# One core, adaLN with linear attention and an MLP: block 1's rows transposed by VectorE and DRAM

## The chip, the cores and the metric

The kernel runs on one core of a Trainium2 chip. The metric is the device time of one execution in microseconds (us), the lower the better. It is measured several times; the median counts. Names of engines in the profile: PE (TensorE), DVE (VectorE), ACT (ScalarE), POOL (GpSimd) and SP (SyncE, whose queue issues the kernel's DMAs). PSUM is the memory in which PE leaves its products, in eight banks.

## The reference

The input x has 2048 rows of 512. Everything is fp32. Cut to what matters:

```python
mod = (silu(c) @ w_mod).reshape(1, 6, 1, 512)          # sa, ca, ga, sb, cb, gb
h = layernorm(x) * (1 + ca) + sa
q, k, v = split(h @ wqkv)                              # 32 heads of 16
pq, pk = q @ w_phi, k @ w_phi                          # per head, 16x16
phi = lambda p: concat([softmax(p), softmax(-p)])      # 32 features a head
kv = phi(pk).T @ v;  z = phi(pk).sum(rows)             # over all 2048 rows
o = (phi(pq) @ kv) / (phi(pq) @ z + 1e-6)
x = x + ga * (o @ wo)
h = layernorm(x) * (1 + cb) + sb
x = x + gb * (gelu(h @ w1 + b1) @ w2 + b2)             # F = 1376
```

## The kernel before, in words

**Tiling.** The rows are eight blocks of 256, each held as two halves of 128 rows. PE contracts over partitions, so a block's normalised rows h have to stand transposed, channels on the partitions: 512 channels are four chunks of 128. Every fp32 product is made from three cheaper ones (`mm3`): each operand is split into a high part and a low part, and high·high, high·low and low·high are added up in PSUM. So a 128×512 product over four chunks is twelve matmuls. The transposed block is therefore two tiles, hT0 (high, made by ScalarE) and hT1 (low, made by GpSimd from the affine tile hf minus hT0, in two halves of two chunks each, `h_finish`).

**Stages.** The head (some 24 us) loads the weights, folds the small matrices w_phi into the weights of q and k (`fold` on PE, read out of PSUM by ScalarE as `wq` or `wk` high and by VectorE as the low part), forms the first modulation vectors (`wm`, `prod`, `affine`) and transposes block 0. Then, block by block, the projections pk, pq and pv, the key features ek, and the accumulation pkv of kv over all rows, until about 137 us. Then kv is closed (kvT, zp), the first two blocks go through attention (qp and qT: transposed features; po: attention's product; pw: times wo), and from 190 us on the MLP runs on pairs of blocks (pg: times w1, g: its gelu, py: times w2) with the attention of the next two blocks in between.

**Two ways to transpose.** `ln1_apply(b)` normalises a block and `h_transpose(b)` transposes it and applies the modulation. Which way is taken is set by the constant NT.

- Blocks 0 and 1 (b < NT): PE transposes eight 128×128 tiles into two PSUM banks (tiles named hp), and the affine step reads the banks. For block 1 the affine step is `h_affine`, four ScalarE instructions into hf.
- Blocks 2 to 7 (b >= NT): VectorE transposes the 32×32 blocks of each half (two instructions, xt to nb), four DMAs store nb to a DRAM tensor nt_dram in an order that completes the transpose, one DMA loads it back with the channels on the partitions (hd), and four ScalarE instructions make hf from hd with the affine step.

**What sets the order.** Each engine runs its instructions in program order, and that order is written out. The functions of the kernel don't issue anything: they leave their instructions in queues, one for each step and engine (class `Later`, lines 220 to 241), and the table ISSUE then lists, for each of the kernel's parts, which queue gives its next instruction. So all instructions carry the line 217 in the profile, and tiles tell them apart. Loads and stores go through SP's one queue in the order of that table: an issue that has to wait for its data holds up all issues behind it. A second table, SLOTS, gives each tile its buffer: nineteen numbered buffers of 4 KB a partition, eight PSUM banks, and pairs of small ones. A tile whose buffer was used by another one waits until the last reader of that one is done.

Of the kernel before, what the change touches and what calls it, by code (L numbers as in the profile page):

```python
# [47 lines left out]
    "32eg91ai750d4gf6cf8ehcd187ga30203dh540b52ca0i999hba44571a6i7b8gag3fii0729f4c2fe569d1ehch8d61bg59801c"  # L48
    "7bda51ii68d72i6cc6g44bh676i1ia4e7ah24igi3g908053d78d90d850883efef7g7bbd7b5d5edbfe4id3f8g6f302hbab1ca"
    "gc1d035356268688c6ac633e1e6c0d3h2dffgahfi9f5df3d02gg340052aa2h0f05gc7532d6ggcbhd8g",  # L50
    "bank":
    "3534201077650761644611400766431302014372076341621740122107154521543753631407720101023324531207674567"
    "54567546767640763123523132153152524724605130311550313053514273015015610",
    "st6a": "11101010",
    "sta": "00010101",
    "vea": "01101101",
    "rsa": "01110001",
    "nma": "10111111",
    "dz": "001110010",
    "mxk": "1010101110101010",  # L60
    "smk": "0110010111011011",
    "rck": "1010010111101101",
    "mxq": "10110010",
    "smq": "00000000",
    "rcq": "10100020",
    "den": "00101110",
    "rd": "10111011",
    "st6b0": "10100110",
    "stb0": "10111101",
    "veb0": "10010101",  # L70
    "rsb0": "11001011",
    "st6c0": "01000110",
    "stc0": "10111100",
    "vec0": "00100100",
    "rsc0": "00101000",
    "nmc0": "10010111",
    "st6b1": "11110101",
    "stb1": "10000110",
    "veb1": "11111110",
    "rsb1": "00010101",  # L80
    "st6c1": "10000001",
    "stc1": "10111010",
    "vec1": "00110110",
    "rsc1": "00100101",
    "nmc1": "00000111",
# [3 lines left out]
-init.v -init.p dq.s db.s x0.s dk.s x1.s dk.s dm.s dk.s dm.s si.a bd.v dq.s fq.p s0.v -w2.p oq.a s0.v -w3.p si.v  # L89
-init.v s0.v dk.s s0.v si.v fk.p si.v s0.v dm.s s0.v oq.v s0.g sr.p s1.v n0.v n0.v s1.v n0.a fq.p s1.v n0.v ok.a  # L90
sr.a fk.p s1.v ok.v x.s m.g dm.s m.v h0.p dv.s ok.a fk.p s1.v bg.s s1.v m.v oq.a ok.v m.a m.g m.v h0.p ok.a -w4.p
f.v +x.s s1.g ok.v fq.p m.a n1.v f.a m.v fk.p n1.a f.v dv.s n1.v f.v m.g oq.a pf.p oq.v f.a n1.a f.v ++x.s m.v ok.a
pf.p m.a m.v oq.v m.g f.v h.p s.v f.a fq.p h.a m.v m.a h.p f.v pf.p bg.s h.a s.v +bg.s h.a s.v +bg.s s.v oq.a s.v
m.v s.v f.v s.g +++x.s oq.v f.a bg.g vs.a f.v q1.p n.v +s.v h.a ok.v vs.a n.v vs.v pf.p n.a vs.g ++s.v n.a q0.p k1.v
bg.a n.v n.v +bg.g bg.v n.s pv0.p +s.v n.s f.a +bg.g ++s.v q1.a n.s +bg.a +s.v ++s.v n.s k1.v f.g +bg.a +bg.s ++s.v
++s.v +s.v +s.v ++s.v k0.v f.a pv1.p k0.v f.g +++s.v n.s k1.v ++++x.s +bg.g +s.v k0.v k0.v
""",
    """
pk1.p s.g +s.g n.v n.v bg.v n.a bg.g -k1.v n.a bg.s ++++x.s ++s.v -q0.a +bg.s pk0.p bg.v -k1.a e.v h.a h.a ++s.v
++s.v n.v -k0.a q1.p +n.v bg.v -v1.a +bg.g ++s.v n.v bg.a e.v h.a n.s +n.a n.s -k0.v f.a pv0.p n.s -v0.a f.g n.s h.a  # L100
# [25 lines left out]
pk1.p -k0.v -k1.a --bg.g -k0.v -k1.v pk0.p h.a -v0.v v1.v k1.v -v0.a -k0.g +d0.s h.a k1.v ----e.s h.a h.a f.a -m0.p
--bg.g k0.v f.a -m1.p k1.v m0.p k1.v pv1.p +w1.s -k1.v +w1.s k1.a --v1.v f.g -v1.v k0.v v1.v k0.v f.g k1.v
""",
    """
pk1.p -v1.a -----e.v --k1.g ---bg.a --v1.a -k0.v -k0.a -k1.v pk0.p ----v0.v k1.v +lp0.s -k1.g -k0.v --v1.v --bg.g  # L130
-k0.v -m1.p w1.a k0.v m1.p k1.v -pv0.p w1.a d0.s v1.v k0.v w1.s -k0.g k0.v v0.v k1.v k0.v -v0.v pv0.p w1.g k0.a
-v0.a k0.v w1.g k0.v pv1.p k1.v v0.a +a0.v k1.a v0.v v1.v k1.v k0.g q1.p v1.a k1.v w1.a +a0.v k1.g ---v0.v m0.p
+a0.g m2.p m3.p w1.g kT.a d1.s d1.s z.p z.a kf.p +a0.g q0.p z.a q1.a a0.g q1.p a1.g a0.v -----e.v a0.v --bg.s q2.p
q1.a a1.g +a0.a kf.v a0.v q0.a a1.v q2.p a0.g a1.v a0.g a0.g +a0.g a0.v +a0.v q0.p a1.g a0.g a1.g a0.v a1.g a0.g
a1.v q4.p q0.a --bg.s x0.s q2.a a1.g +a0.g t01.p a1.g +a0.a t01.p t00.p t00.p +a0.v q4.p q4.a a1.g t01.a +a0.v t00.a
t01.a t00.a +a0.g q2.a o01.p q2.s o00.p w1.s t10.p q0.s o00.a t11.p o01.a +a0.g o00.v t10.p t11.p o01.v w00.p t10.a
+a0.v q4.a t11.a q4.s --bg.g +a0.v t10.a t11.a w1.a o11.p la00.v o10.p la00.a -bg.g w01.p x1.s o10.a la00.v o11.a
o10.v la00.v o11.v +a0.g -bg.a la00.v la00.v la00.g w11.p +a0.g la01.v +a0.g w1.g lb00.v la01.a +a0.v la01.v lb00.v
w10.p la11.v w1.s q1.s la01.v lb00.v la11.a la01.v la01.v +lp1.s la01.g w2.s la11.v -bg.g lb01.v q3.p la11.v lb01.v
la10.v +a0.g lb01.v la11.v la10.a lb00.v lb01.v la11.v lb00.g lb01.g q3.p la10.v la11.g lc00.v la10.v lc01.v la10.v  # L140
lc01.a la10.v la10.g lb11.v +a0.g lc00.a lb10.v q3.a y0.p q3.a lb11.v y0.p y0.a +a0.g lb10.v q3.s y0.a y0.v --bg.a
lb10.v y0.v
""",
    """
u0.p -w1.a -lb11.v -lb10.v -lb11.v a0.v -lb10.g -lb11.g u0.p a0.v ---bg.g -lc10.v -lc11.v a0.v a0.s -lc10.a a1.v
a0.s u0.p -lc11.a a0.s a1.v a0.s a1.g -y1.p -y1.p -y1.a u0.p --v0.v a0.v a1.g -y1.a -y1.v a0.s a1.g -y1.v a1.a a0.s
u1.p a0.s a1.g a0.s u1.p -w1.g +lp0.s u.a u.a u1.p u.a u.v a0.s u.a a1.v a0.s -w2.g d.p -w1.s u.a d.p u.v u.a d.p
u.v d.p a1.g a1.a d.p d.p -w2.a a1.v d.p a1.g d.p a1.v d.p x0.s a1.v u1.p -w2.g a1.v o01.p o00.p +a0.v d.p o00.a
a1.g -w2.s o01.a o00.v d.p a1.g a1.g +a0.g u.p a1.v o01.v u.a a1.g a1.g d.p a1.g w01.p a1.v u.a +a0.v u.a -w1.a u.v
u.a -w2.g a1.v d.p la01.v a1.s d.p a1.v la01.a a1.s w00.p u.v +a0.g -w2.a a1.s a1.v a1.s -w2.g la01.v a1.s a1.s  # L150
+a0.a u.p a1.s la00.v a1.s la00.a -w1.g -w2.s la00.v la01.v +a0.g la01.v la00.v la00.v la00.v d.p u.a la01.g la01.v
a1.s d.p u.a a1.s +a0.g d.p u.v u.p lb01.v la00.g +a0.a lb00.v -w2.g lb01.v lb00.v lb00.v d.p lb01.v u.a lb01.v
lb00.v lb01.g d.p -w2.a lb00.g lc01.v u.p lc00.v +a0.v lc01.a -w2.g u.a lc00.a u.v y0.v d.p +a0.g u.a y0.v -w2.s
x1.s o10.p +a0.v -w2.s o11.p y0.s u.a d.p y0.s o10.a +a0.g o11.a y0.s d.p o10.v y0.s o11.v w10.p +a0.v +a0.v +a0.v
# [42 lines left out]
u.a u.a d.p u.a u.a u.a u.v d.p d.p d.p d.p d.p out.v d.p out.s d.p out.v d.p out.s d.p out.v d.p out.s out.v out.v  # L197
out.s out.s
""",
]  # L200
W2A = 6
AHEAD = 4
NT = 2
BUFS = 19
ALIGN = 64
NE = 2


class Held:
# [35 lines left out]
def adaln_hedgehog_mixer(ctx, tc, x, wqT, wkT, wv, wo, w1, w2, b2, wmodT, small_in, out):  # L245
# [164 lines left out]
    def ln1_apply(b):  # L410
# [7 lines left out]

        if b >= NT:
            t = wtile("nb", [16, 2, 32])  # L420
# [751 lines left out]
```

## Time and profile before

| | us |
|---|---|
| median of 3 runs | 470.64 (470.19 to 471.09) |
| profiled execution | 470.68 |
| its span, first to last instruction | 468.9 |
| PE busy | 462.5 |
| DVE, POOL, ACT busy | 314.1, 279.7, 235.6 |
| granted TensorE clock | 0.999 of full speed |

The span is what the instructions of the profiled execution cover; 1.8 us lie outside it. Rows of the profile name a group by engine, operation and tile, out<-in, with the buffer numbers left out. In rows by time the first number is the start in us from the span's start and the second the length. A wait stands in square brackets behind a row, with what ended it. A matmul's shown length is longer than the step from one to the next, since they are pipelined; the chain of work that ended last shows the steps.

### The profile page before, as it was taken

How to read it: one execution, taken by the hardware profiler on the slowest of the kernel's cores; microseconds unless marked ns; L12 is line 12 of the kernel's file. 1: busy time of each engine (PE TensorE's matmuls, PEld its weight loads, DVE VectorE, ACT ScalarE, POOL GpSimd, SP SyncE). 2: the span in 40 equal slices, each digit the busy share in tenths (PEclk: the TensorE clock that was granted, in tenths of full speed). 3: DMA queues.
4: the chain of work that ended last, by engine and by line, in shares of the span. 5: the costliest groups of instructions: out<-in, count | busy, mean ns of one | idle time of the engine just before them, and what ended most of it. 6: DMA issues, size and time to landing. Idle time of an engine off the chain costs nothing.

```text
span 468.9 us, 8567 instructions
## 1 busy us (share of the span) xinstructions
PE 462.5 (99%) x3313; PEld 375.2 (80%) x3313; DVE 314.1 (67%) x610; ACT 235.6 (50%) x383; POOL 279.7 (60%) x233
## 2 busy tenths in 40 slices
PE   9999999999999999999999999999999999999996
PEld 5888888888878878988787878788788788788884
DVE  4999989998848389578885869795873282211113
ACT  2777686855541555758537672166533224422221
POOL 0485859879899989999879975663740010400000
PEclk9999999999999999999999999999999999999999
DMA  8999639636622446937636838168337205100002
GB/s 293 401 263 296 148 78 244 220 65 217 205 64 89 141 174 228 223 112 163 191 97 135 223 113 202 48 110 196 118 76 178 87 0 135 46 22 24 0 1 89
DMA packets 81033, 67.00 MB, mean 143 GB/s; under 512 B 52560, under 2 KB 68320, under 8 KB 80736
## 3 DMA queue, kind: packets, MB, share of 16 engines
q1 hardware_dynamic: 80992, 66.46, 50.1%
q8 instruction: 26, 0.43, 0.4%
q14 instruction: 15, 0.12, 0.1%
HBM read 44.41 MB, written 22.03 MB: 142 GB/s over the span
## 4 chain that ended last, share of the span: by engine, by line
PE 92%; DVE 3%; issue 1%; ACT 1%; DMA 1%; DVEq 0%; ACTq 0%
PE pg L217 26%; PE py L217 26%; PE pv L217 9%; PE pk L217 9%; PE pq L217 7%; PE pw L217 7%; PE warm L217 2%; PE pkv L217 2%; PE fold L217 1%; DVE pw L217 1%; PE po L217 1%; DMA pq_dram<-qs 1%; ACT qT L217 1%; DVE st6c L217 1%; PE zp L217 0%
## 5 line engine op out<-in xcount | busy, mean ns | idle before, releaser
L217 PE MATMUL pg<-yT,w 128*128 128x512 f32 (+1 forms) x528 | 115.5, 370 | 0.7 <-DVE yT L217 0.4
L217 PEld LDWEIGHTS pg<-yT,w 128*128 128x128 f32 x528 | 92.9, 188 | 18.2 <-DVE yT L217 0.6
L217 ACT ACTIVATE pg<-pg,blob 128x512 f32<-128x512 f32 x44 | 29.1, 661 | 106.5 <-PE pg L217 104.3
L217 DVE TENSOR_TENSOR g<-pg,g 128x512 fp32r<-128x512 f32 x40 | 27.2, 684 | 66.9 <-ACT g L217 66.7
L217 PE MATMUL py<-w2a,g 128*128 128x512 f32 x288 | 71.9, 392 | 0.0
L217 PEld LDWEIGHTS py<-w2a,g 128*128 128x128 f32 x288 | 53.5, 188 | 13.4 <-issue 1.6
L217 PE MATMUL py<-w2b,g 128*128 128x512 f32 x192 | 47.2, 390 | 0.0
L217 PE MATMUL pv<-wvh,hT 128*128 128x512 f32 x192 | 45.8, 392 | 0.0
L217 PE MATMUL pk<-wk,hT 128*128 128x512 f32 x192 | 45.6, 391 | 0.0
L217 PE MATMUL pw<-wo,oT 128*128 128x512 f32 x192 | 45.6, 390 | 0.0
L217 PE MATMUL pq<-wq,hT 128*128 128x512 f32 x192 | 45.2, 390 | 0.0
L217 POOL TENSOR_TENSOR ez<-eq,zb 128x1024 f32<-128x1024 f32 x15 | 36.4, 2440 | 13.2 <-PE pg L217 6.1
L217 PEld LDWEIGHTS py<-w2b,g 128*128 128x128 f32 x192 | 35.9, 188 | 8.1 <-issue 0.7
L217 PEld LDWEIGHTS pw<-wo,oT 128*128 128x128 f32 x192 | 35.9, 188 | 7.8 <-issue 0.4
L217 PEld LDWEIGHTS pq<-wq,hT 128*128 128x128 f32 x192 | 35.9, 188 | 7.4
L217 PEld LDWEIGHTS pv<-wvh,hT 128*128 128x128 f32 x192 | 35.7, 188 | 7.5
L217 PEld LDWEIGHTS pk<-wk,hT 128*128 128x128 f32 x192 | 35.8, 188 | 7.3
L217 POOL TENSOR_TENSOR ek<-ek,rck 128x1024 f32<-128x1024 f32 x16 | 31.0, 1947 | 4.3 <-ACT vf L217 1.6
L217 POOL TENSOR_TENSOR eq<-eq,rcq 128x1024 f32<-128x1024 f32 x15 | 28.9, 1939 | 0.2
L217 ACT ACTIVATE g<-pg 128x512 fp32r<-128x512 f32 x40 | 24.0, 599 | 9.5 <-DVE stc L217 2.8
L217 POOL TENSOR_TENSOR rsb<-veb,mhalf 128x1 f32<-128x1 f32 x16 | 8.8, 550 | 30.3 <-DVE veb L217 30.3
L217 POOL TENSOR_TENSOR yT<-yf,yT 128x256 fp32r<-128x256 f32 x24 | 17.1, 744 | 15.2 <-ACT yT L217 15.2
(154 smaller groups left out, 802.4 us busy)
## 6 DMA issues: line engine op xcount, KB each, us to landing
et_dram<-eb SPq DMA_DIRECT2D x48, 128.0 KB, 2.8
eT<-et_dram SPq DMA_DIRECT2D x12, 512.0 KB, 5.5
xt<-in_x SPq DMA_DIRECT2D x8, 512.0 KB, 6.4
wms<-in_wmodT SPq DMA_DIRECT2D x8, 512.0 KB, 5.9
x<-in_x SPq DMA_DIRECT2D x8, 512.0 KB, 3.8
out<-x SPq DMA_DIRECT2D x15, 256.0 KB, 2.1
nt_dram<-nb SPq DMA_DIRECT2D x24, 128.0 KB, 3.3
hd<-nt_dram SPq DMA_DIRECT2D x6, 512.0 KB, 4.2
```

Of the source, the lines that this page charges most:

```text
L217: return lambda *a, **k: self.later.hold(self.letter, lambda: f(*a, **k))
```

## The change

Constant NT goes from 2 to 1: block 1 takes the way through VectorE and DRAM. Its eight PE transposes and their two PSUM banks are gone; two VectorE transposes, four stores and one load are added; its four affine steps read hd in SBUF instead of PSUM. Block 0 is as before. The tables ISSUE and SLOTS, are made anew for the whole kernel; all other constants and all functions are the same.

```diff
 SLOTS = {
     "buf":
-    "32eg91ai750d4gf6cf8ehcd187ga30203dh540b52ca0i999hba44571a6i7b8gag3fii0729f4c2fe569d1ehch8d61bg59801c"
...
+    "78hefif3gadd14b89ch5g84d023f5iec7880c966g4ed167bg3fgbh1h481a26e7b4abi273d510c58b9iefg192126h6i4agd78"
...
 ISSUE = [
     """
-init.v -init.p dq.s db.s x0.s dk.s x1.s dk.s dm.s dk.s dm.s si.a bd.v dq.s fq.p s0.v -w2.p oq.a s0.v -w3.p si.v
...
+-init.v -init.p dq.s db.s x0.s dk.s dk.s x1.s dm.s dm.s si.a bd.v -w2.p dk.s si.v si.v fq.p dq.s si.v s0.v fq.p dm.s
...
-NT = 2
+NT = 1
```

What this does to the order is shown at three places. In the rows a number behind a name is that of the tile.

The first is PE in the head, where the first block's keys (pk) are computed. The piece of the difference begins and ends in that product; hp with xt are block 1's transposes, fold the folded weights of q or k:

```order
 L217 MATMUL pk<-wk,hT_152 128x512 x2
 L217 MATMUL pk<-wk,hT_153 128x512
-L217 MATMUL hp<-blob,xt 128x128 x4
-L217 MATMUL fold<-bd,q 128x128 x4
-L217 MATMUL hp<-blob,xt 128x128 x4
+L217 MATMUL fold<-bd,k 128x128 x4
 L217 MATMUL pk<-wk,hT_152 128x512 x2
 L217 MATMUL pk<-wk,hT_153 128x512
```

Both transposes of block 1 are gone, and another fold stands between the keys' matmuls.

The second is SP in the head. xt is a block of x, wm and wms are modulation weights, wv_s_141 and wv_s_142 the two halves of the weight of v. Before:

```order
L217 DMA wm_139<-in_wmodT 128x1024
L217 DMA wv_s_141<-in_wv 128x1024
L217 DMA wms_168<-in_wmodT 128x1024
L217 DMA xt_202<-in_x 128x2x512
L217 DMA wv_s_142<-in_wv 128x1024
L217 DMA xt_238<-in_x 128x2x512
L217 DMA wms_195<-in_wmodT 128x1024
L217 DMA wms_201<-in_wmodT 128x1024
```

After:

```order
L217 DMA wv_s_141<-in_wv 128x1024
L217 DMA k_140<-in_wkT 128x512
L217 DMA xt_171<-in_x 128x2x512
L217 DMA wm_139<-in_wmodT 128x1024
L217 DMA xt_238<-in_x 128x2x512
L217 DMA wms_170<-in_wmodT 128x1024
L217 DMA nt_dram1_91<-nb_163 32x16x64 x4
L217 DMA wv_s_142<-in_wv 128x1024
L217 DMA wms_195<-in_wmodT 128x1024
L217 DMA xt_202<-in_x 128x2x512
L217 DMA hd_164<-nt_dram1_91 128x4x256
```

The second half of the weight of v now stands behind block 1's four stores, which wait for VectorE's transposes. On VectorE these stand among the small steps of the modulation weights and of block 0's transposed rows:

```order
L217 ISA prod_146,affine_111<-wm_138,scp_145 128x512
L217 ISA affine_111 128x1
L217 STREAM_TRANSPOSE nb_163<-xt_143 128x16x32
L217 TENSOR_TENSOR hT1_153<-hp_150,hT0_152 128x256
L217 TENSOR_SCALAR affine_111<-affine_111 128x1
L217 STREAM_TRANSPOSE nb_163<-xt_143 128x16x32
L217 TENSOR_SCALAR hp_151<-hp_151,affine_111 128x256
```

Two transposes stand there, where before there was none ahead of block 2's.

The third is ScalarE after kv is closed and in the first MLP pair. qT are copies of transposed query features, qs copies of projected queries that are stored to DRAM, oT the attention's output. Before, around 165 us:

```order
L217 ACTIVATE oT0_418<-po_420 128x2x256
L217 ACTIVATE oT0_418<-po_421 128x2x256
L217 ACTIVATE qT_444<-qp_443 128x512
L217 ACTIVATE qs_454<-pq_456 128x512
L217 ACTIVATE qT_459<-qp_458 128x512
L217 ACTIVATE qT_444<-qp_445 128x512
L217 ACTIVATE qT_459<-qp_460 128x512
```

After:

```order
L217 ACTIVATE oT0_418<-po_420 128x2x256
L217 ACTIVATE oT0_418<-po_421 128x2x256
L217 ACTIVATE qs_454<-pq_456 128x512
L217 ACTIVATE qT_444<-qp_443 128x512
L217 ACTIVATE qT_444<-qp_445 128x512
L217 ACTIVATE qT_459<-qp_458 128x512
L217 ACTIVATE qT_459<-qp_460 128x512
```

The copy qs no longer stands between the qT. In the first MLP pair, where eq are exponentials of the query features of the next blocks and pg_517 and g_518 the two steps of the third gelu, the order after is

```order
L217 ACTIVATE g_507<-pg_506 128x512
L217 ACTIVATE pg_508<-pg_508,blob_106 128x512
L217 ACTIVATE g_509<-pg_508 128x512
L217 ACT_TABLE_LOAD
L217 ACTIVATE eq_563<-eq_563 128x1024
L217 ACTIVATE eq_564<-eq_564 128x1024
L217 ACT_TABLE_LOAD
L217 ACTIVATE pg_517<-pg_517,blob_106 128x512
L217 ACTIVATE g_518<-pg_517 128x512
```

Before, eq_563 stood ahead of the first gelu and eq_564 behind the third, each with the table load that it needs.

More of the change, by code (lines that the diff above doesn't have):

```diff
@@ L82 @@
[L82 to L85, printed above, removed]
+    "2723450533675311606216650430512610164323601502264541430157250302615403776441636342637146231504574057"
+    "574074574056243170103703710173171516277034030304734704303017445452454",
+    "st6a": "10110111",
+    "sta": "11101010",
+    "vea": "10001011",
+    "rsa": "10100101",
+    "nma": "11011101",
+    "dz": "001111111",
+    "mxk": "0101011001010101",
+    "smk": "0110100001100010",
+    "rck": "0101100100101000",
@@ new lines @@
+    "mxq": "11000000",
+    "smq": "00000000",
+    "rcq": "21022120",
+    "den": "00001101",
+    "rd": "10100110",
+    "st6b0": "01000101",
+    "stb0": "01110111",
+    "veb0": "11101000",
+    "rsb0": "01001111",
+    "st6c0": "11000010",
+    "stc0": "01000010",
+    "vec0": "11011111",
+    "rsc0": "01000010",
+    "nmc0": "10000011",
+    "st6b1": "11100010",
+    "stb1": "00001100",
+    "veb1": "00000101",
+    "rsb1": "00101110",
+    "st6c1": "11111100",
+    "stc1": "11000000",
+    "vec1": "11010011",
@@ L86 @@
+    "rsc1": "10100010",
+    "nmc1": "11110110",
 }
@@ new lines @@
+bg.g h.a k1.v e.a +n.s pv1.p ++s.v k0.v +n.s f.a -k0.v n.s bg.a f.g +n.s bg.a ++s.v +bg.s +e.v f.a +n.s ++s.g v1.a
+++++x.s f.g
+""",
+    """
+q0.p ++s.v bg.v bg.g -k0.v -k0.v h.a q1.p bg.g +n.v --k0.v bg.a --k1.v h.a e.g bg.a ++s.v bg.v h.a bg.g ++s.v f.a
+pk1.p bg.v n.s -k0.v --k0.g -k1.v -k0.a -k1.v +n.a --v1.v ++s.v --k1.v pk0.p +n.v bg.a bg.v k1.v --k1.g -k1.a +++s.v
++++s.v h.a k1.v f.g +n.a -m0.p +++s.v ++s.v --v1.v e.v -v0.a -m1.p f.a bg.p pv0.p +h.a k1.v f.g +h.a +n.v -k1.v
+++s.g q0.a +f.a k0.v pv1.p q1.a +f.g -k1.v +h.a q1.s +n.v -k1.g k0.v +n.s k0.v +n.s bg.a
@@ new lines @@
+lb10.g lb11.v lb11.v +a0.v lb11.g lc10.v lc10.a xb.g lc11.v lc11.a y1.v d.p u.a y1.v d.p +a1.v y1.s +a0.g u.p +a0.g
+y1.s y1.s u.a y1.s u.a +a0.g +a0.v d.p u.a +a1.v yf0.a d.p u.a u.v d.p yf0.g u.a +a0.v yf0.a d.p +a1.g y1.s u.a u.v
+d.p +a0.s u.a u.a +a1.g yf0.a +a0.s d.p ++lp0.s d.p +a1.g +a0.s d.p +a1.a +a1.g d.p u.a u.a d.p yf0.g u.v yf1.a d.p
+yf0.g yf1.a yf1.a d.p yf1.g yf0.a d.p yf1.a d.p +a1.a yf1.g out.v d.p +a1.v yf1.g d.p out.s +a0.s yf0.g +a0.v yf1.g
+""",
+    """
+u.p a0.v a1.g a1.v a0.s a0.s u.p u.a -out.v a0.s a1.v u.a a0.s -xb.g u.v a1.v d.p u.a d.p a0.s a1.g u.a -out.v
@@ new lines @@
+-out.s d.p u.v a0.s d.p -out.s +a0.v d.p a1.v d.p d.p +a0.v a1.g u.p a1.g a1.g +a0.g a1.v -out.v a1.g -out.s +a0.g
+x0.s d.p u.a +a0.g o00.p u.a o01.p a1.g u.p o01.a o00.a o01.v u.v a1.g a1.v +a0.a o00.v d.p +a0.g w01.p +a0.v +a0.a
+a1.v a1.s +a0.v a1.s w00.p a1.s a1.v u.a a1.s a1.v u.a u.v +a0.g a1.s +a0.v a1.s d.p a1.s d.p a1.s d.p +a0.g +a0.v
+u.p x1.s la00.v +lp1.s la01.v a1.s a1.s xb.g la01.v la00.v d.p u.a la00.v d.p u.a d.p u.v u.p la01.v la01.v +a0.v
+la00.v +a1.v +a0.g d.p u.a la00.v d.p la00.g u.a +a0.g d.p u.v +a0.g d.p +a0.v la00.v +a0.g o11.p la01.v o10.p
@@ new lines @@
+lb11.v lb10.g u.p lb11.g lc10.v lc10.a lc11.v u.a y1.v lc11.a u.v y1.v u.p +a1.v y1.s u.a y1.s +a1.v u.a y1.s y1.s
+u.v d.p y0.s u.a d.p u.a
+""",
+    """
+o01.p o00.p -y1.s a1.g -d.p o00.a -u.a -d.p o00.v a1.v -d.p -yf0.a -d.p o01.a a1.v -yf0.a -d.p -d.p o01.v a1.g
+-yf1.a -yf1.a w00.p -yf0.g -yf0.a -u.a -yf0.a a1.g -u.a -yf0.g -yf1.a -u.a -yf1.a -yf1.g -u.a -yf1.g w01.p -yf1.g
+a1.g -yf1.g a1.v -u.v a1.g -yf0.g -d.p la01.v -d.p -yf0.g u.p la00.v -xb.g la01.v la01.v -out.v -out.s -d.p u.a -d.p
@@ new lines @@
+-out.v u.a u.p -out.s u.v x1.s la00.v la00.v la01.v la00.v la01.v -out.v d.p la01.g u.a la00.v a1.g la00.v u.p u.a
+u.v la00.g a1.v a1.g la01.v d.p u.a d.p u.a d.p a1.v d.p a1.v a1.s d.p u.v a1.s -d.p a1.v -out.s d.p a1.s lb00.v d.p
+a1.s lb00.v d.p a1.s lb00.v lb00.v lb01.v a1.s u.p lb00.g -out.v a1.s lb01.v a1.s lb01.v lb01.v lb01.g d.p u.a d.p
+d.p a1.s a1.s u.p -out.s u.a u.v lc01.v lc00.v d.p u.a d.p lc00.a d.p d.p u.p u.a lc01.a u.v o11.p o10.p d.p o11.a
+u.a d.p o11.v o10.a u.p u.a o10.v w10.p u.a u.a w11.p la10.v u.v la10.v la10.v la10.v d.p la11.v d.p la11.v d.p
@@ new lines @@
+u.p u.p u.a u.a u.v d.p u.a -d.p u.a -d.p -d.p u.v -d.p -out.v u.p -out.v -out.s -out.s d.p u.a d.p u.a d.p u.v d.p
+-d.p d.p d.p u.p d.p u.a d.p u.a d.p u.v d.p -out.v u.p d.p u.a d.p u.a d.p u.v d.p d.p d.p u.p d.p u.a d.p u.a d.p
+u.v u.p d.p u.a d.p u.a d.p u.v d.p -out.v d.p d.p u.p u.p u.a u.a u.v d.p u.a d.p u.a d.p u.v d.p u.p u.p u.a d.p
+u.a d.p u.a u.v d.p u.a u.a d.p u.a u.a d.p u.a u.a u.v d.p d.p d.p d.p d.p out.v d.p out.s d.p out.v -out.s d.p
+out.s d.p out.v -out.s d.p out.s out.v out.v out.s out.s
```

177 lines of the change are left out of this document (58 added, 119 removed).

## The prediction

> **What bounds the kernel now.** I read the busy shares first, then the chain that ended last, then the busy times by stretch, then the matrix engine's waits.
>
> ```profile
> PE 462.5 (99%) x3313; PEld 375.2 (80%) x3313; DVE 314.1 (67%) x610; ACT 235.6 (50%) x383; POOL 279.7 (60%) x233
> PE 92%; DVE 3%; issue 1%; ACT 1%; DMA 1%; DVEq 0%; ACTq 0%
> ```
>
> ```profile
> 10.00:20.00 10.00, 9.91 (x75) 8.90 (x74) 8.94 (x29) 8.01 (x17) 5.43 (x5) 1.00 1.03 405
> 20.00:24.00 4.00, 4.00 (x27) 3.55 (x26) 3.97 (x13) 2.92 (x9) 0.71 (x2) 1.00 1.04 394
> 24.00:134.00 110.00, 110.00 (x1280) 90.89 (x1279) 101.25 (x214) 73.30 (x120) 90.71 (x61) 1.00 0.64 185
> 134.00:190.00 56.00, 54.34 (x518) 44.67 (x517) 38.59 (x71) 26.04 (x44) 52.25 (x43) 1.00 0.48 150
> 190.00:465.00 275.00, 275.00 (x1402) 222.76 (x1400) 157.14 (x272) 123.29 (x194) 129.73 (x121) 1.00 0.42 107
> ```
>
> In the second fence the columns after the length are PE, PEld, DVE, ACT and POOL busy, granted clock, DMA share, GB/s. PE has no gap at all from 24 to 134 us and from 190 to 465, and its clock is whole. So the time is the sum of its matmuls plus the few waits it has, and these are listed:
>
> ```profile
> PE warm L217 <- DVE ones L217: 0.9, 1, 0.9
> PE zp L217 <- ACT kvT L217: 0.5, 1, 0.5
> PE pg L217 <- DVE yT L217: 0.4, 1, 0.4
> PE po L217 <- ACT qT L217: 0.4, 1, 0.4
> PE pg L217 <- ACT yT L217: 0.3, 1, 0.3
> ```
>
> Two things follow. What leaves PE's stream shortens the kernel by its own length, wherever PE stays covered. And every wait that the change brings to PE lengthens it by as much: there is no slack on PE to swallow one. The head, up to 24 us, is also the place where the DMA engines are full (share 1.03 and 1.04 at about 400 GB/s), and there the change puts five more transfers.
>
> **The change, part by part.**
>
> *Eight transposes leave PE.* They stand on the chain that ended last (start, length, what):
>
> ```profile
> 21.25 0.44 PE hp L217 x4
> 21.68 0.89 PE fold L217 x8
> 22.58 0.44 PE hp L217 x4
> 23.01 1.38 PE pk L217 x6
> ...
> 31.19 5.44 PE pv L217 x24
> 36.63 5.44 PE pk L217 x24
> ```
>
> Two groups of four at 0.44 us: 0.88 us, with PE busy on both sides of them, so −0.88. The other PE instructions are the same in number.
>
> *A wait in the head.* The second group of transposes of block 0 shares a PSUM bank with a folded weight that VectorE has to read out first:
>
> ```profile
> 14.05 1.06 PE L217 MATMUL fold<-bd,k 128*128 128x128 f32 x8
> 15.19 0.66 PE L217 MATMUL hp<-blob,xt 128*128 128x128 f32 x4
> 14.44 0.69 DVE L217 TENSOR_TENSOR wk<-fold,wk 128x512 fp32r<-128x512 f32 x1 [0.90 <-ACT wk L217]
> ```
>
> Eight folds take 0.89 us from start to start (the chain's row at 21.68), so PE could have gone on at 14.05 + 0.89 = 14.94; it went on at 15.19, just after VectorE's 14.44 + 0.69 = 15.13. In the new order that fold stands one warm-up matmul and a transpose group further ahead of the reader, and VectorE takes it before a reduction of modulation weights instead of after one: −0.25.
>
> *What the new path costs off PE.* Two stream transposes on VectorE, four stores, one load, and ScalarE's four affine steps from SBUF instead of PSUM:
>
> ```profile
> L217 DVE STREAM_TRANSPOSE nb<-xt x12: 652/700/712, 29.1 to 99.6; 128x512 f32<-128x512 f32 x12
> L217 ACT ACTIVATE hf<-hd,affine x24: 582/589/601, 40.4 to 111.6; 128x256 f32<-128x256 f32 x24
> L217 ACT ACTIVATE hf<-hp,affine x4: 554/563/582, 21.8 to 25.5; 128x256 f32<-128x256 f32 x4
> nt_dram<-nb SPq DMA_DIRECT2D x24, 128.0 KB, 3.3
> hd<-nt_dram SPq DMA_DIRECT2D x6, 512.0 KB, 4.2
> xt<-in_x SPq DMA_DIRECT2D x4, 512.0 KB, 7.9
> 30.44 2.21 SPq L217 DMA_DIRECT2D nt_dram<-nb  x4
> ```
>
> (the DMA rows end with the median from issue to landing; that of xt is for 10 to 34 us alone, where the engines are full). ScalarE pays 4 × 0.026 = 0.1 us: nothing, since it idles in the head. VectorE pays about 1.3 us, covered only while its results are early. The path is a chain of its own, and I lay it out with times of before:
>
> ```profile
> 18.89 0.68 DVE L217 CUSTOM_DVE_ANT_0 prod<-wm,scp 128x512 f32<-128x512 f32 x1
> 32.69 2.73 POOL L217 TENSOR_TENSOR hT<-hf,hT 128x512 fp32r<-128x512 f32 x2
> 27.06 3.19 POOL L217 TENSOR_TENSOR wvh<-wv_s,wvh 128x1024 fp32r<-128x1024 f32 x1 [1.52 <-ACT wvh L217]
> 25.90 1.09 ACT L217 ACTIVATE wvh<-wv_s 128x1024 fp32r<-128x1024 f32 x1
> 16.34 0.47 SPq L217 DMA_DIRECT2D wv_s<-in_wv  x1
> ```
>
> The transposes follow the reduction of 18.89. A weight step of about 0.7 us that ran ahead of it is now later, so it starts near 18.2; with it (0.68), both transposes (1.3) and half a microsecond of small steps between, they end near 20.7. SP then issues four stores in 2.21 us, until 22.9; the last one, issued at 22.4, lands 3.3 later, at 25.7. The load hd starts there. It took 4.2 us where the DMA engines were at 0.64; loads of its size took 7.9 where they were full. At 25.7 one or two loads of 512 KB are still ahead of it, 1.3 us each at 400 GB/s: I take 4.2 + 1.3 = 5.5, so 31.2 (ends of the range 29.9 and 33.6). Then for the first half two affine steps (1.2), ScalarE's high part (0.6) and GpSimd's low part (1.3): 34.3; the second half at the latest 31.2 + 4 × 0.59 + 2 × 0.62 + 1.3 = 36.1. PE wants the first half when block 1's pk begins, 36.63 − 0.88 − 0.25 = 35.5, and the second six matmuls (1.36 us) later, 36.9. Slack 1.2 and 0.8 us: I count nothing. If the cover is gone, each microsecond costs one.
>
> The Trainium skill (DMA: Bandwidth & Descriptors, Anatomy of one DMA) fits a transfer as 2.0 us plus its bytes at 436 GB/s, for DMAs that GpSimd issues; an estimate by that page is 2.3 us for a store and 3.2 for the load, and by it hd would land near 27.9, with over 4 us of slack and the first rival below gone. The rows of this kernel, 3.3 and 4.2 on SP's queue and 7.9 where it is full, are longer, and they decide.
>
> *What is queued behind the stores.* SP stands still from the loads ahead until the transposes are done, and behind the stores waits the second half of the weight of v. Issued at 16.34 before, it was in SBUF by 25.90 (about 25.0, I take it, since ScalarE was busy with the first half until then); cast 1.09, low part on GpSimd 3.19, done at 30.25, first pv at 31.19. The same loads stand ahead of it now plus 512 KB of stores, 1.3 us: 26.3, cast 27.4, low part 30.6. PE reaches that half six matmuls after its first pv, at 31.19 − 1.13 + 1.36 = 31.4. Slack 0.8, cost nothing, the bounds 0 and, if the load is a full 7.5 to 7.9 us from its issue at 22.9, (22.9 + 7.9 + 1.1 + 3.2) − 31.4 = 3.7.
>
> *The order of the later stages.* It is another order throughout, and two places in it change a wait. At 166 us PE waits for the transposed features qT, which ScalarE copies in an order that has one of its own copies waiting for a store:
>
> ```profile
> 162.15 3.04 SPq L217 DMA_DIRECT2D pq_dram<-qs  x2
> 165.79 1.57 ACT L217 ACTIVATE qT<-qp 128x512 f32<-128x512 f32 x3 [0.95 <-DMA pq_dram<-qs]
> 163.53 3.01 PE L217 MATMUL pw<-wo,oT 128*128 128x512 f32 x12
> 166.93 1.37 PE L217 MATMUL po<-qT,gab 64*32 64x256 f32 x25 [0.39 <-ACT qT L217]
> ```
>
> In the new order the two copies of the stored queries come before, and four qT stand in a row with buffers free: the wait at po goes. The list has 0.4 for it; from start to start it is more, since pw's twelve matmuls at 0.227 (1.36 / 6, the chain's row of 23.01 has 1.38) end their turns at 166.25 and po starts at 166.93, 0.68. I take the middle, −0.55 (bounds 0 and −0.68). Against it, in the first MLP block ScalarE does two exponentials and two table loads ahead of the third gelu, where only the first exponential stood before:
>
> ```profile
> 192.62 1.28 ACT L217 ACT_TABLE_LOAD   x1 [0.81 <-PE pg L217]
> 198.88 1.06 ACT L217 ACTIVATE eq<-eq 128x1024 f32<-128x1024 f32 x1
> ```
>
> 2 × 1.28 + 2 × 1.06 = 4.7 us in which that gelu is late. PE has other groups of the same block to run; I take 0.3 us of wait there, between 0 and 1.3 (a table load more than the cover), and 0.2 for the MLP's exp tiles, which come back from DRAM near the time of use. The waits at zp (0.5) and at yT (0.4 and 0.3) I leave, their producers being the same. The key side gains nothing and loses slack:
>
> ```profile
> 64.66 0.71 DVE L217 STREAM_TRANSPOSE nb<-xt 128x512 f32<-128x512 f32 x1 [1.52 <-PE pkv L217]
> ```
>
> This is VectorE's only long idle time there; with 1.3 us more work on VectorE and PE 1.1 earlier it is used up. VectorE is at 101.25 of 110 us, so I count 0, with up to 1 as the bad end.
>
> **The sum.** The profiled execution took 470.68 us (span 468.9 and 1.8 around it), 0.04 over the median of 470.64. 470.68 − 0.88 − 0.25 − 0.55 + 0.3 + 0.2 = 469.5. A measurement of this kernel can tell about 0.2% from no change, 0.94 us; so 469.70 is the border to faster, and the forecast lies just beyond it.
>
> **The rivals.**
>
> *Block 1's way through DRAM is late (slower).* Place: the head, PE at block 1's first pk or at the second half of pv. It decides from hd landing later than about 32.1, or the weight of v later than 27.1. For it: the engines at 1.03 to 1.04, 7.9 us for loads there, a slack of 0.8 us. Against it: the medians 3.3 and 4.2. With hd at 33.6 the second half is ready at 38.5 against 36.9, at the worst order of ScalarE: +1.6. Then 469.5 + 1.6 = 471.1; with the weight of v late as well up to 3.7, 473.2. I centre it on 471.9. The Trainium skill (VectorE: DVE Perf Modes, The three transpose paths, and its rules for kernel authors) points to this side: VectorE transposes only separate 32×32 blocks, and for 128×128 it advises TensorE where PSUM will do. The trace agrees that the way round is longer, 1.3 us and five transfers against 0.88 us; it differs in that the longer way is not on the engine that binds.
>
> *The gain is filled up again (no change).* The freed 1.1 us of the head only brings PE sooner to the waits at zp, yT and po, whose producers GpSimd (52.25 of 56 us in that stretch) and VectorE set. Then zp, po and yT together grow by what the head gives: 470.68 − 1.13 + 1.1 = 470.65. For it: GpSimd nearly full there. Against it: GpSimd's chain there starts from what PE delivers earlier.
>
> *The new order waits elsewhere (slower).* The prior order held PE without a gap for 110 and 275 us, with many transfers landing within 1 us of use, and VectorE keeps next to no reserve on the key side. Two or three places late by 0.5 to 1 us give 469.5 + 2.5 = 472.
>
> **How the numbers follow.** Forecast 0.46 (own range 468.6 to 470.3, some 0.38 of it under 469.70), filled up again 0.19, DRAM late 0.13, new waits elsewhere 0.22. Faster 0.38, within 0.2% 0.08 + 0.19 = 0.27, slower 0.35. The range reaches from 468.4 (yT's waits go as well, 469.5 − 0.7, and the 0.3 and 0.2 don't come) to 473.2 (the head's bad end), which leaves out about 0.2.
>
> **What the new profile would show.** No hp row after 20 us; two nb in the head near 19 to 21; PE at pv near 30.1 and at block 1's pk near 35.5 with no wait named. If the DRAM way is late, the waits list has pk for hT or pv for wvh, with hd landing after 32. The po wait should be gone; a py or pg wait for g near 197 to 200 would be the 0.3. If PE's busy time from 24 to 134 or 190 to 465 is short of the stretch by over 1 us, the third rival was right.

## The result and the profile after

| | before | after |
|---|---|---|
| median | 470.38 us (469.54 to 471.09, 13 runs) | 471.36 us (470.04 to 472.8, 13 runs) |
| ratio | | 1.0022 (95% interval 1.0012 to 1.0032) |
| profiled execution, span | 470.68, 468.9 | 470.92, 469.1 |

The change made the kernel slower by 0.2%, about 1 us, where 0.9 us faster was forecast. The profiled executions are only 0.24 us apart, and the two traces show where they part. First the page and the stretches of the changed kernel, in the columns used above (PE, PEld, DVE, ACT and POOL busy, clock, DMA share, GB/s):

```profile
PE 461.0 (98%) x3305; PEld 372.8 (79%) x3305; DVE 317.6 (68%) x612; ACT 232.1 (49%) x379; POOL 278.7 (59%) x233
```

```profile
24.00:134.00 110.00, 109.99 (x1279) 90.37 (x1277) 101.43 (x216) 73.33 (x121) 92.48 (x62) 1.00 0.66 197
134.00:190.00 56.00, 53.38 (x516) 43.93 (x515) 40.21 (x70) 26.40 (x44) 50.07 (x42) 1.00 0.49 161
190.00:465.00 275.00, 274.86 (x1398) 221.96 (x1397) 158.17 (x272) 119.21 (x190) 129.49 (x121) 1.00 0.41 104
```

PE has 8 instructions less and 1.5 us less busy time. It still has next to no gap in the long stretches; most of what it lost, it lost between 134 and 190 us, where it was busy for 53.38 us instead of 54.34. PE's waits name the place:

```profile
PE qp L217 <- POOL eq L217: 1.5, 1, 1.5
PE warm L217 <- DVE ones L217: 0.9, 1, 0.9
PE kvp L217 <- ACT kvT L217: 0.6, 1, 0.6
PE pg L217 <- DVE yT L217: 0.3, 1, 0.3
PE pg L217 <- ACT yT L217: 0.2, 1, 0.2
PE pk L217 <- ACT hT L217: 0.2, 1, 0.2
```

The wait at po is gone, as forecast. The first row is new: PE waits for the scaled query features eq of GpSimd, to transpose them (qp). (The last row is block 0's, at 18.9 us.) The chain that ended last shows block 1's start and what stands ahead of the wait at qp (start, length, what):

```profile
29.80 5.67 PE pv L217 x24
35.46 2.79 PE pk L217 x12
...
145.29 3.46 DVE ez L217
148.75 2.27 DVE dz L217 x2
...
154.00 2.88 POOL eq L217
156.93 1.86 PE qp L217 x15
```

pv starts at 29.80 instead of 31.19 and block 1's pk at 35.46 instead of 36.63: PE is 1.17 us ahead. It is still ahead at the end of kv, where ScalarE's copy kvT starts 1.18 us earlier. Before and after (by time, ScalarE):

```profile
137.35 0.38 ACT L217 ACTIVATE kvT<-pkv 128x256 f32<-128x256 f32 x1 [3.08 <-issue]
```

```profile
136.17 0.38 ACT L217 ACTIVATE kvT<-pkv 128x256 f32<-128x256 f32 x1 [1.14 <-PE pkv L217]
```

But this lead does not come from block 1's transposes. The chain's first rows, before and then after, where warm are matmuls on a tile of ones whose product nothing reads, and scp spreads a vector over the partitions:

```profile
0.92 6.67 PE warm L217 x8
7.59 0.89 PE fold L217 x8
8.48 1.72 PE warm L217 x4
10.20 0.89 PE fold L217 x8
11.09 0.89 PE scp L217 x8
```

```profile
0.92 6.29 PE warm L217 x10
7.20 2.68 PE fold L217 x24
9.88 0.89 PE scp L217 x8
```

Ahead of scp stands as much work in both (two warm less and eight folds more, 0.86 and 0.89 us), and after the change it starts 1.21 us earlier: the lead was there at 10 us, ahead of block 1's transposes. The four warm matmuls at 8.48 take 0.43 us each, the first eight twice as long on average, and how long the first ones take differs from execution to execution. In the old head the eight took 6.67 us here and 5.26 in another execution (that of the third experiment below, which has the same head); in the new order ten took 6.12 to 6.59 us in seven profiled executions and 7.41 and 7.45 in two.

Twenty us behind kvT the lead is lost. On the chain stands VectorE's product ez (query features times the key sum), 3.46 us for one instruction. The view of tile ez, first before, then after (minimum, median and maximum in ns):

```profile
L217 POOL TENSOR_TENSOR ez<-eq,zb x15: 2370/2395/3011, 140.5 to 328.3; 128x1024 f32<-128x1024 f32 x15
L217 DVE TENSOR_TENSOR ez<-eq,zb x1: 1395/1395/1395, 144.9 to 144.9; 128x1024 f32<-128x1024 f32 x1
```

```profile
L217 POOL TENSOR_TENSOR ez<-eq,zb x15: 2382/2398/2408, 139.5 to 326.4; 128x1024 f32<-128x1024 f32 x15
L217 DVE TENSOR_TENSOR ez<-eq,zb x1: 3465/3465/3465, 145.3 to 145.3; 128x1024 f32<-128x1024 f32 x1
```

The same instruction on the same shape took 1.40 us and then 3.46. What differs is what GpSimd did meanwhile. After, by time, VectorE and then GpSimd:

```profile
144.15 1.22 DVE L217 TENSOR_REDUCE smq<-eq 128x64 f32<-128x1024 f32 x1
145.29 3.46 DVE L217 TENSOR_TENSOR ez<-eq,zb 128x1024 f32<-128x1024 f32 x1
```

```profile
142.92 4.76 POOL L217 TENSOR_TENSOR ez<-eq,zb 128x1024 f32<-128x1024 f32 x2
```

GpSimd's two products ran from 142.92 to 147.68, the second from about 145.3. VectorE's started in the same moment and ended 1.07 us after GpSimd's: it stood still for most of the time that GpSimd worked. Before, VectorE's product started at 144.93 (row in the view above), 0.3 us before one of GpSimd's ended, was done at 146.3, and the next one of GpSimd's had to wait instead: it is the maximum of 3011 ns, 0.6 above the median. The reduction smq, with one input, ran at its usual 1.22 beside GpSimd's product. In the old order no reduction stood ahead of ez; in the new one smq does, and puts it 1.1 us later, into GpSimd's next product. The later sums dz, GpSimd's small steps behind them and eq, for which PE waits, all come about 2 us later, counted from kvT, and GpSimd's eq itself took 2.91 us instead of 1.94, beside VectorE's product eq. Before, and then after:

```profile
153.01 1.94 POOL L217 TENSOR_TENSOR eq<-eq,rcq 128x1024 f32<-128x1024 f32 x1
```

```profile
153.88 1.21 DVE L217 TENSOR_TENSOR eq<-eq,rcq 128x1024 f32<-128x1024 f32 x1
153.96 2.91 POOL L217 TENSOR_TENSOR eq<-eq,rcq 128x1024 f32<-128x1024 f32 x1
```

The two profiled executions side by side, in starts (us; the first two from the chain, the others by time):

| | before | after | difference |
|---|---|---|---|
| scp in the head | 11.09 | 9.88 | −1.21 |
| block 1's pk | 36.63 | 35.46 | −1.17 |
| kvT | 137.35 | 136.17 | −1.18 |
| pq behind the first qp | 157.88 | 158.54 | +0.66 |
| pw behind the last po | 168.44 | 168.19 | −0.25 |
| PE's last matmul | 464.52 | 464.26 | −0.26 |
| VectorE's last product | 465.18 | 464.93 | −0.25 |
| end of the span | 468.9 | 469.1 | +0.2 |

From kvT to the pq 1.8 us are lost, 1.7 of them at qp from start to start, and the po place gives back 0.9. PE's last matmul still starts 0.26 us earlier than before; the span is longer because 3.4 us instead of 3.0 pass behind the end of VectorE's last product, where only stores are left. Why isn't shown: in nine other profiles that stretch took 2.9 to 3.5 us. Had the warm matmuls taken as long as before, this execution would have lost up to 1.4 us (an estimate, 0.24 + 1.21); the medians say 1.0.

### The profile page after: what moved, and what is told of

Same layout as the page of the kernel before. It is cut to its first block, busy times and chain, and to the rows that moved or that the text cites. A ratio compares the mean times of both kernels' runs of the same rounds, so it can differ in the third digit from the quotient of the medians.

```text
span 469.1 us, 8561 instructions
## 1 busy us (share of the span) xinstructions
PE 461.0 (98%) x3305; PEld 372.8 (79%) x3305; DVE 317.6 (68%) x612; ACT 232.1 (49%) x379; POOL 278.7 (59%) x233
## 4 chain that ended last, share of the span: by engine, by line
PE 90%; DVE 5%; POOL 2%; issue 1%; ACT 1%; DVEq 0%; ACTq 0%
PE pg L217 26%; PE py L217 26%; PE pv L217 9%; PE pk L217 9%; PE pw L217 8%; PE pq L217 5%; PE pkv L217 2%; PE warm L217 2%; PE po L217 2%; DVE pw L217 1%; PE fold L217 1%; POOL eq L217 1%; PE qp L217 1%; DVE dz L217 1%; DVE ez L217 1%
## 5 line engine op out<-in xcount | busy, mean ns | idle before, releaser
L217 PE MATMUL py<-w2a,g 128*128 128x512 f32 x288 | 70.8, 391 | 0.0
```

The lines of the kernel that those rows point to most:

```text
L217: return lambda *a, **k: self.later.hold(self.letter, lambda: f(*a, **k))
```

## The experiments

Theory A is the one just told, as it stood when the runs were made: the head's gain is real and is eaten by a collision of two products in the new order. Theory B: GpSimd simply has too much to do there. Theory C: the loss is in block 1's way through DRAM, late in some executions. Theory D came later and is a milder C: that way has no slack, so that PE waits for block 1's hT in some executions.

**The changed kernel, once more.** No edit.

> The changed kernel as it is, to see its profile a second time. Theory A (the gain of the head, 1.2 us, is eaten at 155 us, where PE waits for GpSimd's eq because VectorE's product ez fell together with GpSimd's ez): qp waits 1.2 to 1.8 us again, VectorE's ez takes 3 us or more, time 471.0 to 471.8. Theory C (the loss is not at qp; block 1's way through DRAM is late in some executions): another profile shows a wait at pk or pv in the head of 0.5 us or more, and qp waits less.

471.48 us (12 runs), ratio 1.0025 (1.0016 to 1.0034). Its profiled execution took 471.65 us, 0.7 more than the first one. The rows of PE's waits that the first one did not have, and PE at block 1's pk:

```profile
PE pk L217 <- POOL hT L217: 0.3, 1, 0.3
PE po L217 <- DMA eT<-et_dram: 0.2, 1, 0.2
PE pq L217 <- POOL hT L217: 0.2, 1, 0.2
```

```profile
34.60 2.15 PE L217 MATMUL pk<-wk,hT 128*128 128x512 f32 x8
37.07 1.19 PE L217 MATMUL pk<-wk,hT 128*128 128x512 f32 x4 [0.33 <-POOL hT L217]
```

The wait of 1.5 us at qp is there too. So the collision is in both, and there is some of C: in this execution PE began block 1 at 34.60, 0.7 earlier than in the first (35.30 in this view), and had to wait for the second half of hT, which GpSimd finished at 37.01 as in the first (36.99). What the head gains beyond that is lost at once. At kvT its lead over before is down to 0.71 us, and its last matmul starts at 464.95, 0.43 later than before.

**VectorE's product first.** In the changed kernel VectorE's two reductions smq go behind the sums of the first two blocks and behind its product eq:

```diff
 L217 RECIPROCAL rcq<-smq 128x128
-L217 TENSOR_REDUCE smq<-eq 128x64
 L217 TENSOR_TENSOR ez<-eq,zb 128x1024
 L217 TENSOR_REDUCE dz<-ez 128x64 x3
...
 L217 TENSOR_REDUCE smq<-eq 128x64
 L217 TENSOR_TENSOR eq<-eq,rcq 128x1024
+L217 TENSOR_REDUCE smq<-eq 128x64
```

> The changed kernel with two of VectorE's reductions smq put later, so that its product ez starts at 144.1 us and not at 145.3. Theory A: ez takes 2.4 us or less instead of 3.46 and ends near 146.4, the wait at qp falls from 1.5 to under 0.3, time 1.4 to 1.7 us less than the changed kernel, 469.7 to 470.0. Theory B (GpSimd has too much to do there in its new order, whatever VectorE does): qp still waits over 1 us, time within 0.4 us of the changed kernel. Theory C: time as the changed kernel's.

469.32 us (12 runs), ratio to before 0.9981 (0.997 to 0.9993): 2.2 us below the changed kernel on the same chip. PE's waits, all of them, and VectorE's product with GpSimd's two beside it:

```profile
PE warm L217 <- DVE ones L217: 0.9, 1, 0.9
PE kvp L217 <- ACT kvT L217: 0.6, 1, 0.6
PE pg L217 <- DVE yT L217: 0.5, 1, 0.5
PE pg L217 <- ACT yT L217: 0.3, 1, 0.3
```

```profile
143.13 2.44 DVE L217 TENSOR_TENSOR ez<-eq,zb 128x1024 f32<-128x1024 f32 x1
```

```profile
142.08 5.75 POOL L217 TENSOR_TENSOR ez<-eq,zb 128x1024 f32<-128x1024 f32 x2
```

The wait at qp is gone. VectorE waited from 143.13 for GpSimd's first product, had its turn, and GpSimd's second waited for it (5.75 for two instead of 4.76). GpSimd has the same work in the same order, so B is out. The gain is above the 1.4 to 1.7 expected. Between the profiled executions it is 2.1 us from kvT (135.33 against 136.17) to the last matmul (461.32 against 464.26); the other 0.84 us came ahead of kvT, where the edit changes nothing. The edit takes away two things at once, the 1.1 us of the reduction and 1.0 us of standing still, and the run doesn't part them. GpSimd's eq, 2.93 us here, is as slow as in the changed kernel and without a wait.

**The collision made in the kernel before.** One reduction, and the exponential that it reads, go ahead of VectorE's product:

```diff
 L217 RECIPROCAL rcq<-smq 128x128
+L217 TENSOR_REDUCE smq<-eq 128x64
 L217 TENSOR_TENSOR ez<-eq,zb 128x1024
 L217 TENSOR_TENSOR gab<-kvp,blob 128x256
 L217 TENSOR_REDUCE dz<-ez 128x64 x3
 L217 RECIPROCAL rd<-den 128x64
-L217 TENSOR_REDUCE smq<-eq 128x64
```

> The kernel before, with the same collision made in it: VectorE's reduction smq (and the exponential that it needs) goes ahead of its product ez, which so starts near 146.1 us, while GpSimd is in its third ez. Theory A: ez takes 2.8 to 3.6 us instead of 1.4, PE waits 0.7 to 1.2 us at qp, where it did not, time 471.1 to 471.6. Theory B: the work is the same, VectorE only has it in another order, so no wait and 470.4.

471.59 us (5 runs), ratio 1.0037 (1.0024 to 1.005), 1.4 us slower than before. VectorE's product and PE at qp:

```profile
145.61 2.80 DVE L217 TENSOR_TENSOR ez<-eq,zb 128x1024 f32<-128x1024 f32 x1
```

```profile
156.52 1.86 PE L217 MATMUL qp<-blob,eq 128*128 128x128 f32 x15 [0.68 <-POOL eq L217]
```

The product at 2.80 and the wait came as A says. From kvT (136.72, 0.63 earlier than before) to the last matmul (465.44, 0.92 later) it loses 1.55 us: 0.9 of it at qp, start to start, and the rest at po, which waits for ScalarE's qT (0.9 in two waits instead of 0.4); the edit moves an exponential on ScalarE too. Put in, the reduction costs 1.4 us; taken out of the new order, it gave 2.2.

The lengths of VectorE's ez, 1.40, 2.44, 2.80 and twice 3.46 us in the five profiles so far, follow from GpSimd's product beside it: VectorE's ended 1.07 to 1.13 us after GpSimd's in all five, whether it had started 0.3 us ahead of that end (before) or 2.4 (after).

**The change alone.** The kernel before with NT = 1, two buffers for nb and hd, and only the head's order changed, by hand: VectorE's transposes stand in place of two readouts of folded weights, and block 2's statistics come later.

```diff
-NT = 2
+NT = 1
...
 L217 TENSOR_SCALAR hp_150<-hp_150,affine_111 128x256
-L217 TENSOR_TENSOR wq_121<-fold_170,wq_121 128x512
+L217 STREAM_TRANSPOSE nb_163<-xt_143 128x16x32
 L217 TENSOR_TENSOR hT1_153<-hp_150,hT0_152 128x256
```

> The kernel before with block 1 by way of DRAM, and its old order kept from 60 us on: only the head is rearranged by hand. Theory A: the head's gain is kept to the end, block 1's pk starts at 35.3 to 36.0 us, no wait at qp, 469.2 to 469.8. Theory C (the way through DRAM itself costs): PE waits 0.5 us or more at pk or pv in the head and the time is 470.4 to 471.4.

479.12 us (4 runs), ratio 1.0189: both theories missed by far. PE waits for a fold's bank that VectorE read too late (1.9 us), and then for the copies qs and vf, ahead of which ScalarE stood 3.8 us for VectorE's step nma of the later statistics, and 2.3 us for a later block's hd:

```profile
45.34 4.35 PE L217 MATMUL pq<-wq,hT 128*128 128x512 f32 x12 [2.06 <-ACT qs L217]
51.09 2.10 PE L217 MATMUL pv<-wvh,hT 128*128 128x512 f32 x8 [1.40 <-ACT vf L217]
```

These are waits of my order and don't tell A from C. It shows only that VectorE's 1.3 us and the load that ScalarE waits for don't fit into the old head by this rearrangement.

**Block 1 back on PE, in the new order.** The kernel of the second experiment with NT = 2; the eight transposes stand between the two halves of block 0's pq, the transposes on VectorE, stores and load are gone.

```diff
-NT = 1
+NT = 2
...
 L217 MATMUL pq_197<-wq_121,hT1_153 128x512
+L217 MATMUL hp_171<-blob_106,xt_143 128x128 x4
+L217 MATMUL hp_173<-blob_106,xt_143 128x128 x4
 L217 MATMUL pq_198<-wq_121,hT0_152 128x512 x2
```

> The kernel of the first experiment with block 1's transposes back on PE (between the two halves of pq of block 0), its stores and its load gone, the later order untouched: what the way through DRAM is worth by itself. Prediction's theory (0.88 us of PE, on the path): 0.7 to 0.9 us above the first experiment, 470.0 to 470.3, and no wait for block 1's hT. Theory D (in most executions PE waits for block 1's hT, so that the way through DRAM gives back most of what it saves): 0 to 0.4 us above, 469.3 to 469.7.

469.74 us (11 runs), ratio 0.9988 (0.9978 to 0.9999). The second experiment's kernel beside it (no edit)

> The first experiment's kernel again, on the chip of these runs, to compare with: 469.0 to 469.7, no wait at qp. Theory D: its profile shows block 1's pk waiting for hT if PE starts block 1 before 34.9 us.

had 469.41 us (12 runs), ratio 0.9984 (0.9972 to 0.9996). That is 0.33 us for the way through DRAM, in D's range, but the intervals are wider than what separates D from the forecast 0.88. This is not settled. The profiled execution of the latter started block 1 at 34.48 us and did not wait for hT, against D. That with block 1 on PE started it at 35.64, its warm matmuls having taken as long (6.39 us against 6.45). Against the three profiled executions of the second experiment's kernel (34.48, 34.52 and 34.84) that is 0.8 to 1.2 us, which fits the 0.88. But it also waits 0.5 us for a later block's hT, at 113 us, where the others don't wait at all: the order was made for the way through DRAM, and part of the 0.33 can be that.

**hd earlier.** In the second experiment's kernel hd goes ahead of a load of x and one of modulation weights, and ScalarE's second high part of block 1 ahead of a copy of v:

```diff
 L217 DMA wv_s<-in_wv 128x1024
-L217 DMA wms<-in_wmodT 128x1024
+L217 DMA hd<-nt_dram_91 128x4x256
 L217 DMA xt<-in_x 128x2x512
-L217 DMA hd<-nt_dram_91 128x4x256
```

> The kernel of the first experiment with block 1's load hd issued ahead of two loads that it stood behind, and ScalarE's second high part of block 1 ahead of a copy of v. Theory D: hd lands near 29.5 us instead of 31.1 to 31.8, no wait at block 1's pk whatever the start, time 0.3 to 0.6 us below the first experiment, 468.7 to 469.0, with less spread. Prediction's theory (slack in the head already, nothing to gain): within 0.2 us of it.

470.27 us (12 runs), ratio 0.9993 (0.9981 to 1.0006): no gain, rather a loss of 0.9 us against 469.41, against both theories. In its profile the weight of v is what is late:

```profile
32.35 0.96 PE L217 MATMUL pv<-wvh,hT 128*128 128x512 f32 x3 [0.74 <-POOL wvh L217]
```

**hd later.** One more load of 512 KB ahead of it:

```diff
 L217 DMA xt<-in_x 128x2x512
+L217 DMA wms<-in_wmodT 128x1024
 L217 DMA hd<-nt_dram_91 128x4x256
-L217 DMA wms<-in_wmodT 128x1024
```

> The kernel of the first experiment with one more load of 512 KB ahead of block 1's load hd. Theory D (block 1's way through DRAM has no slack left in the head): hd lands 1.2 to 1.5 us later, near 32.5 to 33, PE waits 0.8 to 1.5 us at block 1's pk for hT, time 0.5 to 1.2 us above the first experiment's 469.3 to 469.4. Prediction's theory (0.8 us of slack): a wait of 0.5 us or less, time within 0.4 us.

470.62 us (11 runs), ratio 1.0008 (0.9999 to 1.0017); the second experiment's kernel in the same session (no edit)

> The first experiment's kernel once more, to compare with on the chip of these runs: 469.0 to 469.7.

had 468.72 us (5 runs), ratio 0.997 (0.9958 to 0.9982). So 1.9 us against it here, and 1.2 to 1.3 against the earlier two medians. PE in the head:

```profile
32.03 4.17 PE L217 MATMUL pv<-wvh,hT 128*128 128x512 f32 x17 [0.44 <-POOL wvh L217]
36.03 0.61 PE L217 MATMUL pk<-wk,hT 128*128 128x512 f32 x2
37.03 1.66 PE L217 MATMUL pk<-wk,hT 128*128 128x512 f32 x6 [0.39 <-POOL hT L217]
39.03 1.20 PE L217 MATMUL pk<-wk,hT 128*128 128x512 f32 x4 [0.34 <-POOL hT L217]
```

Both halves of hT are waited for, though PE reached block 1 at 36.03, 0.7 later than in the changed kernel (35.30), after slow warm matmuls (7.41 us). ScalarE's first step on hd starts at 33.87, 2.0 us later than in the changed kernel and 2.6 to 3.0 later than in the second experiment's three executions, more than the 1.2 to 1.5 meant: the loss is not the price of 512 KB alone. The slack can be read without the edit. PE takes eight matmuls of block 1 before it needs the second half of hT (the row at 34.60 of the first experiment; eight at 0.227 are 1.82 us). GpSimd finished that half 0.1 to 0.3 us before this moment in four profiled executions, and 0.6 after it in the one that waited. The way through DRAM had no 0.8 us to spare: D.

**A load of x later.** In the second experiment's kernel the load of a later block's rows, ahead of block 1's stores, goes behind hd, and its first statistics later with it:

```diff
-L217 DMA xt<-in_x 128x2x512
 L217 DMA wms<-in_wmodT 128x1024
 L217 DMA nt_dram_91<-nb 32x16x64 x4
...
 L217 DMA hd<-nt_dram_91 128x4x256
+L217 DMA xt<-in_x 128x2x512
```

> The kernel of the first experiment with the load of a later block's rows (and its first statistics) moved from ahead of block 1's stores to behind hd: weight of v, stores and hd then have 512 KB less ahead of them. Theory D: stores, weight of v and hd land about 1.3 us earlier (hd near 30), no wait in the head whatever the start, time 0.3 to 0.8 us below the first experiment. Prediction's theory: within 0.2 us.

469.72 us (12 runs), ratio 0.9985 (0.9975 to 0.9995): no better than the second experiment's kernel, which had 468.72 beside it. There was no wait in the head of the profiled execution, but there was none in that of its neighbour without the edit either; a wait for the MLP's exp tiles (0.4 us, po for eT) stood later. So D does not explain why the kernels with the new order spread over 1.4 to 3.6 us from run to run (468.0 to 471.2 for the second experiment), where the kernel before spreads over 1.2 to 2.2. Up to 1.4 us of a spread can be the warm matmuls, in both orders. The execution that was profiled was the fastest of its kernel in three of these (468.01, 467.91 and 468.22 us), so that the waits of the slower ones were not seen, except in the second profile of the changed kernel. The rest stays open.

## Why the prediction was wrong

*Eight transposes, −0.88, and the head's wait, −0.25:* the sum, 1.13 forecast and 1.18 measured at kvT, agrees by luck. 1.21 us of lead stood at scp, from the warm matmuls, and between scp and block 1 this execution gained nothing: it lost again in the head what the transposes and the wait gave. The transposes themselves are borne out by the executions with like warm matmuls, 0.8 to 1.2 us at block 1 (block 1 back on PE); how much of it reaches the end is open (0.33 us between medians). The wait at hp is a term of one execution: 0.25 us before, start to start, 0.8 in the third experiment, which has the same head. The times of the head came within 0.6 us, with the same luck: pv at 29.80 (30.1), block 1's pk at 35.46 (35.5), hd, whose first affine step is the next row, at 31.8 (31.2).

```profile
31.87 1.10 ACT L217 ACTIVATE hf<-hd,affine 128x256 f32<-128x256 f32 x2 [1.73 <-DMA hd<-nt_dram]
35.69 1.30 POOL L217 TENSOR_TENSOR hT<-hf,hT 128x512 fp32r<-128x512 f32 x1
```

*"Slack 1.2 and 0.8 us: I count nothing":* mis-sized. hT's first half was complete at 35.00, not 34.3, and the second at 36.99, not 36.1: hd came 0.6 us later than forecast, and a copy of v stood ahead of ScalarE's second high part. PE wants the second eight matmuls after block 1's start and not six, 35.30 + 1.82 = 37.12 by time, so its slack was 0.1 us. One execution of the changed kernel waited 0.3 us for it at block 1, and 0.2 for block 2's at 53.95. The first rival was half right: it named the place.

*The wait at po, −0.55:* right in kind and small in size. Its row is gone, and not only because PE waits ahead of it now: with the collision away PE's list has neither qp nor po for qT. From the table above the place was worth 0.9 us: po's own 32 matmuls took 1.58 us before and 1.09 after, and the bound of 0.68 counted only their start.

*+0.3 for a gelu and +0.2 for exp tiles:* the gelu's did not come; PE was busy for 274.86 of 275.00 us in the MLP. The tiles' 0.2 is in the second profile of the changed kernel and not in the first.

*"The waits at zp and at yT I leave, their producers being the same":* this step failed. I took the attention's start to be as long as before, because the same instructions stand in it, and earlier, because it starts from PE. The instructions were the same; their order and their lengths were not. A reduction of 1.1 us came to stand ahead of VectorE's product, the product went from 1.40 to 3.46 us and GpSimd's eq from 1.94 to 2.91, and the wait at qp of 1.5 us (1.7 from start to start), which the sum does not have, took more than the lead. The third rival (the new order waits elsewhere) happened, at one place and not in small pieces. The second rival (filled up again, 470.65) comes near the profiled 470.92 by luck: it had GpSimd too full, and with the same work in the same order on GpSimd the gain came. (The lower end of the range, 468.4, is 468.3 by its own terms.) The row that would have told was in the profile of before: GpSimd's ez with a median of 2395 ns and a maximum of 3011, at the very moment of VectorE's product. The Trainium skill states the rule (SBUF — State Buffer, Who interferes with whom): a VectorE instruction with two inputs in SBUF and a GpSimd instruction that reads SBUF share a port, and whichever comes second stands still until the other is done. The traces agree, with 2.1 us of standing still on VectorE here and 0.6 to 1.0 on GpSimd. With the rule one would have gone through the new order for such pairs.

With the two reductions moved the kernel takes 469.3 us, close to the 469.5 forecast, and is faster than before by 0.2 to 0.3% (0.9981, 0.9984 and 0.997 in three sessions). That does not prove the forecast's terms: part of it is the po place, which gave more than forecast, and the way through DRAM by itself is not settled. Of the median's loss of 1 us the wait at qp is the part that is shown; what the slower executions wait for beside it stays open.

The Trainium skill's advice to transpose 128×128 on TensorE (VectorE: DVE Perf Modes, Rules for kernel authors) would have given the right sign, for a reason that the runs do not show: with the collision away, the way through DRAM was not slower than block 1 on PE in the same order (469.41 against 469.74, the intervals overlapping).

## What to carry to other kernels

When an order is made anew, the durations of the old trace are not yet those of the new one: look in the old profile for instructions whose longest time is far above the median, find what ran beside them, and look for such pairs in the new order ahead of each engine that PE waits for. Where PE is the bound, what leaves its stream is a gain only up to the next producer that is just in time; a slack of 0.8 us worked out from medians was 0.1 in the trace. Before a lead between two traces is put down to a change, compare them at a mark ahead of the change: here the whole lead of 1.2 us was there at 10 us. A new order can be repaired at one row: the wait, followed back along the chain, names the instruction that stood too late.

## What the runs showed of the hardware

Products with two inputs in SBUF on VectorE and on GpSimd took turns: VectorE's ended 1.07 to 1.13 us after GpSimd's in five profiles, and took 1.40 to 3.46 us for it. Reductions with one input ran beside GpSimd's products at their usual 1.2 us. And in the kernel with the change alone, PE's granted clock fell after a wait of 2.06 us. The stretches behind it, in the columns used before (the clock is the third number from the end):

```profile
45.00:47.00 2.00, 1.66 (x7) 1.33 (x8) 2.00 (x7) 1.24 (x2) 1.16 (x1) 0.93 0.85 224
47.00:49.10 2.10, 2.10 (x7) 1.60 (x5) 2.10 (x8) 0.58 (x2) 0.13 (x1) 0.50 0.87 309
```

The twelve matmuls of that wait's row took 4.35 us, where twelve of the same shape take 2.88. So this wait cost 1.5 us more than its own length. A wait of 1.94 us in the same execution and the 1.5 us at qp left the clock at 1.00 behind them; what decides is not shown by one case.
